# A searched order of all tasks for an attention and MoE kernel, planned with later landings, and a fifth buffer for exponentials

## The chip and the metric

One NeuronCore of one Trainium2 chip runs the whole program: TensorE (PE in the views; its weight loads PEld), VectorE (DVE), ScalarE (ACT), and SyncE (SP), which issues every transfer here. The metric is the device time of one execution in microseconds (us), lower is better. A measurement of this kernel can tell about 0.5% from no change.

## What is computed

Two batches, eight heads, 768 positions, head size 64: attention within clusters. Each query and key goes to the centroid with the largest normalised product, and a score counts only where both have the same cluster. Then two feed-forward blocks over all 1536 rows.

```python
mask = q_assign[:, :, :, None] == k_assign[:, :, None, :]
scores = np.where(mask, scale * np.matmul(q, k.transpose(0, 1, 3, 2)), -1000000000.0)
attn = softmax(scores)                       # written out in the reference
x = np.matmul(attn, v)                       # then to (1536, 512)
h = x @ w_in                                 # (1536, 2048)
g = (a0 + a1*h + a2*h**2 + a3*h**3) / (1 + abs(b0)*abs(h) + abs(b1)*h**2 + 1e-6)
x = g @ w_out                                # (1536, 512)
out = ((x @ w1) * (x @ w2) @ w3) @ wo2       # (1536, 512)
```

## The kernel before

The arithmetic comes in blocks. **FirstW** and the four **w_block**s multiply w3 by wo2 in fp32 (lines 620 and 636). An attention **unit** is one head and one tile of 128 queries, 96 in all: four score matmuls into a score bank `s` (line 844, two of them with a residual and the mask as extra rows), the row maximum on DVE (L852), the exponential on ACT into a buffer `E` (L853), six transposes on PE into two banks `t` (L866) and two copies by ACT into `et` (L872). After six units `av` multiplies by v (L906), scales on DVE (L912) and writes the head to `xd` in DRAM, from where `p1_block` loads it as `x`. The rows are treated in three chunks of 512: **p1** (eight blocks per chunk, x by w_in; L575 in fp32 for the first chunk, L577 to L579 as three fp32r matmuls for the others), the rational function behind it on ACT and DVE (L696 to L710, reading the bank `s`), **p2** (by w_out), **p3** (by w1 and w2) and **p4** (by the product W). Weights arrive as 64-bit numbers and are decoded into fp32 by one ACT and three DVE instructions (L482 to L486), then split in two fp32r parts (L526 on ACT, L527 on DVE), and some are stored in DRAM (`fin`, `fout`, `f`) for the next chunk. Cluster masks take four passes (`one`): logits on PE (L436), a transpose, a maximum, a comparison, a transpose on DVE (L442 to L445), a count on PE (L450), a last DVE step (L454).

Nothing of the order is written by hand. Every instruction or small group is a `Task` with an engine, an assumed cost and a priority. `Plan.forward` plays the four engines' queues with those costs and with assumed lags between engines; on SP a transfer takes its place behind the others, lands, and is counted as there 0.65 us after its data have moved. `Plan.backward` makes ranks from the played schedule, and `Plan.order` repeats both some 20 times, keeps the shortest, and sorts the tasks by their start. Each engine then runs its tasks strictly in that order. Buffers of a class (`SLOTS`: six `w`, three `raw`, four `E`, two `s`, two `t`, one `x`, one `kqr` and so on) are handed out in the planner too, and a task that needs a buffer waits for the last user of the one before it. In the order below, a matmul in fp32 is one row, while the trace shows it as two instructions.

Of the kernel before, what the change touches and what calls it, by code (L numbers as in the profile page):

```python
# [25 lines left out]
    PT=(33.3, 58.0),  # L26
# [5 lines left out]
    AT=(0.3751, 2.75, 3.5, 4.0, 4.0, 4.0, 4.0),  # L32
    M1=0,
    LEAD=(438.6, -178.7, 600.9),
    ALEAD=(-89.5, 241.2),
    MLEAD=2554.6,
    AOFF=37.1,
    SLOTS={"w": 6, "raw": 3, "y": 3, "x": 1, "x2": 2, "g": 16, "et": 3, "E": 4, "kqr": 1, "AB": 2, "v": 1, "sm": 6, "nn": 3, "s": 2, "t": 2, "m": 2, "sums": 2},
    WO2=-2657.8,
    OFF=(-326.5, -317.6, -25.0, -476.0, -310.4, -431.8, 243.3),  # L40
    T0=-1084.3,
    M0=-458.0,
    AHEAD=2,
    W2=("x2", "x2"),
    WR=("x", "x", "w", "w", "raw", "et", "et", "w"),
    WT=("w", "raw"),
    ROUNDS=20,
)
# [77 lines left out]
class Plan:  # L126
# [59 lines left out]
    def forward(self, rank, queue):  # L186
# [34 lines left out]
        while (best := self.next_line(lines)) is not None:  # L221
# [17 lines left out]
    def backward(self):  # L239
# [39 lines left out]
    def order(self, rounds):  # L279
        bufs = [b for q in self.queue.values() for b in q]  # L280
        queue = self.queue
        rank = [t.prio for t in self.tasks]
        best = old = None
        for k in range(rounds + 1):
# [7 lines left out]
            if best is None or span < best[0]:  # L292
                best = span, [(t.start, t.end) for t in self.tasks], [b.slot for b in bufs]
            rank = self.backward()
            old = queue
            if k % 3 == 0:
                first = {b: min(rank[t.i] for t in b.users) for b in bufs}
                queue = {c: sorted(q, key=first.get) for c, q in self.queue.items()}
        if best is None:
            raise RuntimeError("the tasks cannot be placed")  # L300
        for t, (start, end) in zip(self.tasks, best[1]):
            t.start, t.end = start, end
        for b, slot in zip(bufs, best[2]):
# [5 lines left out]
def kernel(  # L309
# [273 lines left out]

    def w_out_part(o, m, at):

        wt = [Buf(cfg["WT"][i], [P, 512], F32R) for i in range(2)]
        op("ACT", 0.48, lambda: nc.scalar.copy(wt[0].t, o.t), [o], [wt[0]], at)
        op("DVE", 0.6, lambda: nc.vector.tensor_tensor(wt[1].t, o.t, f32(wt[0].t), ALU.subtract), [o, wt[0]], [wt[1]], at)
# [4 lines left out]
    class FirstW:  # L593
# [18 lines left out]
        def run(self):  # L612
            at = self.at
            o = [Buf(c, [P, 512]) for c in "mmtt"]
            for j in range(8):
                for m0 in (0, 2):

                    def q(j=j, m0=m0):
                        for m in (m0, m0 + 1):
                            nc.tensor.matmul(o[m].t, self.f[j].t[:, m * P:(m + 1) * P], w2[j][0].t[:, w2[j][1]],  # L620
                                             start=j == 0, stop=j == 7)

                    op("PE", 1.74, q, [self.f[j], w2[j]], o[m0:m0 + 2], at + 3.4 * j)
# [3 lines left out]
    def w_block(m):  # L627
        blk = Blk("D", lambda: w3t_d[m])

        def run():  # L630
            at = blk.at
            o = Buf("m", [P, 512])

            def q(j0):
                for j in range(j0, j0 + 2):
                    nc.tensor.matmul(o.t, blk.f.t[:, j * P:(j + 1) * P], w2[j][0].t[:, w2[j][1]], start=j == 0, stop=j == 7)

            for j0 in range(0, 8, 2):
                op("PE", 1.74, lambda j0=j0: q(j0), blk.reads([j0 * P]) + w2[j0:j0 + 2], [o], at)
# [8 lines left out]
    def p1_block(c, mp):  # L648
        blk = moe_blk(c, "in", mp, lambda: win_d[mp])

        def run():
# [17 lines left out]
            h = Buf("s", [P, 2, 512])  # L669

            def q(mi, k0):
                for k in range(k0, k0 + 2):
                    mm(h.t[:, mi, 0:TC], blk, k * 256 + mi * P, [t[k][2]() for t in xs[c]], k == 0, k == 3)

            for mi in range(2):
                for k0 in (0, 2):
                    op("PE", blk.cost(2), lambda mi=mi, k0=k0: q(mi, k0),
                       blk.reads([k0 * 256]) + [t[k][:2] for t in xs[c] for k in (k0, k0 + 1)], [h], at)
# [3 lines left out]
            def A():  # L682
                return T.t[:, 0]

            def U():
                return T.t[:, 1]
# [4 lines left out]
            def hh():  # L691
                return h.t[:, :, 0:TC]

            tA, tU, tW = (T, 0), (T, 1), V
            s, v = nc.scalar, nc.vector
            op("ACT", act(2 * TC, -0.015), lambda: s.activation(A(), hh(), AF.Abs), [h], [tA], at)  # L696
            op("ACT", act(2 * TC, 0.17), lambda: s.activation(U(), hh(), AF.Identity, bias=neg[:, 2:3], scale=neg[:, 3:4]), [h], [tU], at)
            op("ACT", act(2 * TC, 0.12), lambda: s.activation(W(), A(), AF.Abs, scale=abc[:, 5:6]), [tA], [tW], at)
            op("DVE", dve(2 * TC), lambda: v.tensor_tensor(U(), U(), hh(), ALU.mult), [h], [tU], at)
            op("DVE", dve(2 * TC, 0.06), lambda: v.scalar_tensor_tensor(U(), U(), abc[:, 1:2], hh(), ALU.subtract, ALU.mult), [h], [tU], at)  # L700
            op("DVE", dve(2 * TC, 0.06), lambda: v.scalar_tensor_tensor(W(), W(), b0abs, A(), ALU.add, ALU.mult), [tA], [tW], at)
            op("ACT", act(2 * TC, 0.12), lambda: s.activation(A(), W(), AF.Ln, bias=c1), [tW], [tA], at)
            op("ACT", act(2 * TC, 0.03), lambda: s.activation(A(), A(), AF.Exp, scale=-1.0), [], [tA], at)
            op("DVE", dve(2 * TC), lambda: v.scalar_tensor_tensor(W(), W(), 1.0 + 1e-6, A(), ALU.add, ALU.mult), [tA], [tW], at)
            op("DVE", dve(2 * TC, 0.06), lambda: v.scalar_tensor_tensor(U(), U(), abc[:, 0:1], A(), ALU.subtract, ALU.mult), [tA], [tU], at)
            G = g[c, mp] = operand("out", "g", [P, 2, TC], c)
            if len(G) == 1:
                op("DVE", dve(2 * TC), lambda: v.scalar_tensor_tensor(G[0].t, W(), 2.0, U(), ALU.subtract, ALU.mult), [tW, tU], [(G[0], 0)], at)
# [399 lines left out]
```

## Time and profile before

| | us |
|---|---|
| median of 3 runs | 793.04 |
| lowest, highest | 792.76, 795.72 |
| the profiled execution | 796.5 |
| its span, first to last instruction | 794.6 |
| PE busy | 759.0 |
| DVE busy | 587.4 |
| ACT busy | 509.2 |

The profiled execution is one more run of the same program, 3.5 us above the median. A busy PE in the views includes matmuls that overlap at their ends, so the time that a matmul takes in a full queue is read from the distance of two starts, and waits that are shorter than such an overlap show no idle time.

### The profile page before, as it was taken

What the parts mean: (1) busy time and instruction counts of PE and PEld (TensorE: products, weight loads), DVE (VectorE), ACT (ScalarE), POOL (GpSimd) and SP (SyncE); (2) the same over time, 40 slices, a digit from 0 to 9 for tenths busy, and PEclk for the clock granted to TensorE, in tenths of its full rate; (3) what the DMA queues carried; (4) which work ended last, traced back from release to release, by engine and by line L of the source; (5) the groups of instructions that cost most, each with busy time, mean ns of one, the idle gap of its engine ahead of it and who ended that gap; (6) DMA issues with size and microseconds to landing.
All of it is one profiled execution on the core that took longest, in us unless ns stands there. A gap on an engine that the chain in (4) does not pass through costs nothing.

```text
span 794.6 us, 9724 instructions
## 1 busy us (share of the span) xinstructions
PE 759.0 (96%) x3545; PEld 551.1 (69%) x3545; DVE 587.4 (74%) x731; ACT 509.2 (64%) x827; POOL 0.7 (0%) x6
## 2 busy tenths in 40 slices
PE   1899999999999999999999998999999999999998
PEld 0336577666556556677778877888888888888886
DVE  6897886698788988898658999992379899233420
ACT  3238887988788886988836767862278786223320
POOL 0000000000000000000000000000000000000000
PEclk9799999999999999999999999999999999999999
DMA  7988676488735524428553644733233245332342
GB/s 273 387 278 301 204 254 189 141 244 263 249 123 173 186 94 150 127 61 283 154 190 110 189 150 138 285 116 103 80 106 107 79 156 167 128 102 84 106 158 106
DMA packets 49727, 134.99 MB, mean 170 GB/s; under 512 B 5392, under 2 KB 18448, under 8 KB 49680
## 3 DMA queue, kind: packets, MB, share of 16 engines
q1 hardware_dynamic: 49680, 134.37, 51.2%
q8 instruction: 28, 0.46, 0.2%
q14 instruction: 19, 0.16, 0.1%
HBM read 106.56 MB, written 24.64 MB: 165 GB/s over the span
## 4 chain that ended last, share of the span: by engine, by line
PE 57%; DVE 8%; ACT 6%; DMA 6%; issue 2%; SPq 0%; ACTq 0%; DVEq 0%
PE m L577 12%; PE m L578 12%; PE m L579 12%; PE s L575 4%; PE s L844 3%; PE s L577 3%; PE s L579 3%; PE s L578 3%; PE t L866 3%; PE t L906 3%; DMA raw<-in_w_in_dram 2%; ACT E L853 1%; DMA xd<-E 1%; ACT et L696 1%; DVE et L700 1%
## 5 line engine op out<-in xcount | busy, mean ns | idle before, releaser
L527 DVE TENSOR_TENSOR w<-w,w 128x1024 fp32r<-128x1024 f32 x64 | 78.1, 1222 | 76.0 <-ACT w L526 75.1
L852 DVE TENSOR_REDUCE sm<-s 128x1 f32<-128x768 f32 x96 | 90.7, 952 | 19.7 <-PE s L844 19.2
L526 ACT CAST w<-w 128x1024 fp32r<-128x1024 f32 x64 | 67.1, 1051 | 55.6 <-DMA w<-fout 39.2
L872 ACT COPY et<-t 128x384 f32<-128x384 f32 x192 | 87.8, 506 | 15.7 <-PE t L866 14.0
L844 PE MATMUL s<-AB 80*128 80x384 f32 (+1 forms) x384 | 93.2, 367 | 4.1 <-ACT E L853 2.9
L853 ACT ACTIVATE E<-s,sm 128x768 f32<-128x768 f32 x96 | 89.3, 932 | 7.9 <-DVE sm L852 5.0
L866 PEld LDWEIGHTS t<-ident,E 128*128 128x128 f32 x576 | 68.6, 140 | 27.8 <-issue 11.4
L866 PE MATMUL t<-ident,E 128*128 128x128 f32 x576 | 84.3, 274 | 2.4 <-ACT et L872 2.3
L577 PE MATMUL m<-g,w 128*128 128x512 f32 x192 | 77.4, 403 | 0.0
L844 PEld LDWEIGHTS s<-AB 80*128 80x128 f32 (+1 forms) x384 | 63.6, 189 | 18.7 <-ACT E L853 8.9
L579 PE MATMUL m<-x,w 128*128 128x512 f32 x192 | 75.6, 393 | 0.4 <-DVE w L527 0.4
L577 PE MATMUL m<-x,w 128*128 128x512 f32 x192 | 75.9, 395 | 0.0
L578 PE MATMUL m<-g,w 128*128 128x512 f32 x192 | 75.7, 394 | 0.0
L579 PE MATMUL m<-g,w 128*128 128x512 f32 x192 | 75.5, 393 | 0.0
L578 PE MATMUL m<-x,w 128*128 128x512 f32 x192 | 75.5, 393 | 0.0
L575 PE MATMUL s<-x,w 128*128 128x512 f32 x128 | 58.7, 596 | 3.8 <-DMA x<-xd 1.7
L482 ACT ACTIVATE y<-raw 128x512 f32<-128x512 f32 x65 | 44.9, 694 | 27.4 <-DMA raw<-in_w3t_dram 8.4
L577 PE MATMUL s<-x,w 128*128 128x512 f32 x128 | 50.4, 393 | 2.3 <-DVE et L700 2.3
L579 PE MATMUL s<-x,w 128*128 128x512 f32 x128 | 50.3, 393 | 0.0
L486 DVE SCALAR_TENSOR_TENSOR w<-raw,y 128x512 uint32<-128x512 uint32 x64 | 43.1, 685 | 4.2 <-PE s L575 3.0
L484 DVE SCALAR_TENSOR_TENSOR y<-raw,y 128x512 uint32<-128x512 uint32 x65 | 44.4, 687 | 0.9
L483 DVE TENSOR_SCALAR y<-y 128x512 uint32<-128x512 uint32 x72 | 30.1, 420 | 17.5 <-ACT y L482 17.2
(128 smaller groups left out, 1363.2 us busy)
## 6 DMA issues: line engine op xcount, KB each, us to landing
kqr<-in_kq_dram SPq DMA_DIRECT2D x16, 768.0 KB, 6.2
w<-fout SPq DMA_DIRECT2D x24, 512.0 KB, 3.4
raw<-in_w3t_dram SPq DMA_DIRECT2D x16, 512.0 KB, 6.4
raw<-in_w_out_dram SPq DMA_DIRECT2D x16, 512.0 KB, 5.5
raw<-in_w_in_dram SPq DMA_DIRECT2D x16, 512.0 KB, 5.3
raw<-in_w_dram SPq DMA_DIRECT2D x16, 512.0 KB, 5.5
w<-fin SPq DMA_DIRECT2D x16, 512.0 KB, 3.3
w<-f SPq DMA_DIRECT2D x16, 512.0 KB, 3.2
```

What stands on the lines that cost most here:

```text
L482: op("ACT", 0.52, lambda: nc.scalar.activation(y.t, r.t[:, :, 1].bitcast(F32), AF.Abs, scale=2.0 ** -112), [r], [y], pr)
L526: op("ACT", 0.95, lambda: nc.scalar.copy(self.hi.t, f32(f.t)), words, [self.hi], psp)
L527: op("DVE", 1.135, lambda: nc.vector.tensor_tensor(self.lo.t, f32(f.t), f32(self.hi.t), ALU.subtract), words + [self.hi], [self.lo], psp)
L575: nc.tensor.matmul(o, w.f.t[:, sl], x[0], start=first, stop=last)
L577: nc.tensor.matmul(o, w.hi.t[:, sl], x[0], start=first, stop=False)
L578: nc.tensor.matmul(o, w.hi.t[:, sl], x[1], start=False, stop=False)
L579: nc.tensor.matmul(o, w.lo.t[:, sl], x[0], start=False, stop=last)
L844: nc.tensor.matmul(p.t[:, f, 0:TA], lhs.t[0:n, q0:q0 + P], lhs.t[0:n, k0:k0 + TA], start=st, stop=not st)
L852: op("DVE", 0.865, lambda: nc.vector.tensor_reduce(mx.t, p.t[:, :, 0:TA], axis=AX.XY, op=ALU.max, negate=True), [p], [mx], OF[1])
L853: op("ACT", 0.88, lambda: nc.scalar.activation(E.t, p.t[:, :, 0:TA], AF.Exp, bias=mx.t, accum_out=sums.t[:, i, j:j + 1]), [p, mx], [E, (su ...
L866: nc.tensor.transpose(t.t[:, n * P:(n + 1) * P], e[:, kt * P:(kt + 1) * P], ident)
L872: lambda t=t, lot=lot, v=on_dve: (nc.vector.tensor_copy if v else nc.scalar.copy)(et.t[:, 3 * lot:3 * lot + 3, i * P:(i + 1) * P], t.t[:, ...
```

## The change

The planner gets three edits and the configuration new numbers. A transfer counts as there 1.5 us after its data have moved, where it was 0.65 (and 2.85 for 2.0 in `backward`); a score group on PE costs 0.78 us in the plan, where it was 0.71; `E` has five buffers, where it had four. After the old iteration a search follows: for each number in `SEEDS` (39 of them) the ranks of tasks in a stretch of the plan are shifted at random (`nudged`), the schedule is played again, and a shorter one is kept. PSUM banks are now named by tables (`HC`, `PS`); with the values given these are the banks used before. No arithmetic instruction is added or taken away.

```diff
-    PT=(33.3, 58.0),
+    PT=(8.1, 40.4),
-    AT=(0.3751, 2.75, 3.5, 4.0, 4.0, 4.0, 4.0),
+    AT=(0.75, 2.625, 3.5, 4.0, 4.0, 4.0, 4.0),
-    SLOTS={"w": 6, "raw": 3, ..., "et": 3, "E": 4, "kqr": 1, ...},
+    SLOTS={"w": 6, "raw": 3, ..., "et": 3, "E": 5, "kqr": 1, ...},
...
+    HC=("s", "s", "s"),
+    PS={"W4": "mmtt", "W": "m", "2": "mmm", "3": "mmm", "4": "mmm"},
...
                 dma = max(dma, at + 1.35) + t.nbytes / 360e3
-                t.end = dma + 0.65
+                t.end = dma + 1.5
...
-                r = at + (all_ if all_ < 8 else 2.0 + move)
+                r = at + (all_ if all_ < 8 else 2.85 + move)
...
+    def nudged(self, best, seed):
+        c = [self.chance(i, seed) for i in range(7, 12)]
+        a = c[4] * 60 - 10 if c[3] < 0.4 else c[0] * 600
+        n = (40, 120, 400, 15)[int(c[1] * 3.999)]
+        by = (4, 12, 40, 120, 1)[int(c[2] * 4.999)]
+        return [r + by * (self.chance(i, seed) - 0.5) if a <= best[3][i][0] < a + n else r
+                for i, r in enumerate(best[1])]
...
+        for seed in seeds:
+            other = self.search(self.nudged(best, seed), best[2], 3)
+            if other is not None and other[0] < best[0]:
+                best = other
...
-            op("PE", 0.71, smm, ...)
+            op("PE", 0.78, smm, ...)
```

In the changed kernel all line numbers are some 30 to 46 higher: L656 is the old L620, L672 L636, L604 L575, L890 L844, L912 L866, L740 and L739 are L697 and L696, L555 L526.

**The start, on PE.** The first rows of the program, FirstW into four banks (m and t) over eight slices of the contraction; x_129 and x_122 hold wo2's slices. Before:

```order
L620 MATMUL m_134<-x_129,w_118 128x512
L620 MATMUL m_135<-x_129,w_118 128x512
L620 MATMUL m_134<-x_129,w_140 128x512
L620 MATMUL m_135<-x_129,w_140 128x512
L620 MATMUL m_134<-x_129,w_157 128x512
L620 MATMUL m_135<-x_129,w_157 128x512
L410 MATMUL t_230<-ident,E_146 128x128
```

Now:

```order
L656 MATMUL m_158<-x_122,w_154 128x512
L656 MATMUL m_159<-x_122,w_154 128x512
L656 MATMUL m_158<-x_122,w_141 128x512
L656 MATMUL m_159<-x_122,w_141 128x512
L439 MATMUL t_196<-ident,E_116 128x128
L656 MATMUL m_158<-x_122,w_131 128x512
L656 MATMUL m_159<-x_122,w_131 128x512
L656 MATMUL t_208<-x_122,w_154 128x512
L656 MATMUL t_207<-x_122,w_154 128x512
L465 MATMUL s_217<-g_120,ct 32x384
```

The first pair used to need the first decoded weight and now needs the fourth, w_154; the first mask logits (L465, the old L436) stand behind eight matmuls, where they stood behind ten.

**The first block of p1, on PE.** s_1998 and s_2079 are the bank of p1's first block; the second of its row groups reads the heads that were written to DRAM last. Before, the first row shown is the seventh below the last matmul of `av` for head 7 of the first batch; the six between are two score groups and four groups of transposes:

```order
L636 MATMUL m_1966<-x_129,w_1646 128x512 x2
L844 MATMUL s_1976<-AB_1622 128x384 x4
L866 MATMUL t_1984<-ident,E_1957 128x128 x3
L866 MATMUL t_1994<-ident,E_1957 128x128 x3
L575 MATMUL s_1998<-x_978,w_1593 128x512 x2
L866 MATMUL t_2011<-ident,E_1972 128x128 x3
L866 MATMUL t_2017<-ident,E_1972 128x128 x3
L844 MATMUL s_2023<-AB_1766 128x384 x4
L575 MATMUL s_1998<-x_978,w_1593 128x512 x4
```

Now the first row shown is the tenth below that matmul; the nine between are two score groups, six groups of transposes and a pair of weight matmuls:

```order
L890 MATMUL s_2024<-AB_1796 128x384 x4
L912 MATMUL t_2035<-ident,E_1941 128x128 x3
L912 MATMUL t_2040<-ident,E_2018 128x128 x3
L890 MATMUL s_2044<-AB_1796 128x384 x4
L672 MATMUL m_2009<-x_122,w_1727 128x512 x2
L912 MATMUL t_2069<-ident,E_1996 128x128 x3
L912 MATMUL t_2075<-ident,E_2018 128x128 x3
L604 MATMUL s_2079<-x_953,w_1588 128x512 x2
L936 MATMUL t_2092<-ident,y_2054 128x128 x3
L912 MATMUL t_2098<-ident,E_1996 128x128 x3
L890 MATMUL s_2105<-AB_1796 128x384 x4
L604 MATMUL s_2079<-x_953,w_1588 128x512 x2
```

More work has moved between that `av` and p1's second group of two matmuls, a second pair of weight matmuls (m_2009) and one more score group among it, and that second group is cut in two.

**The sixth p1 block of the second chunk, on ACT.** s_4212 before and s_4210 now are the score bank of that block, which the eighth block takes over. Before:

```order
L698 ACTIVATE raw_4325<-et_4080,abc 128x1024
L526 CAST w_4330<-w_4279 128x1024
L482 ACTIVATE y_4339<-raw_4286 128x512
L697 ACTIVATE et_4341<-s_4212,neg 128x1024
L482 ACTIVATE y_4351<-raw_4307 128x512
L696 ACTIVATE et_4341<-s_4212 128x1024
L702 ACTIVATE et_4080<-raw_4325,c_81 128x1024
```

Now:

```order
L555 CAST w_4308<-w_4293 128x1024
L813 COPY y_4320<-m_4257 128x512
L742 ACTIVATE raw_4322<-et_4094,abc 128x1024
L740 ACTIVATE et_4332<-s_4210,neg 128x1024
L555 CAST w_4341<-w_4283 128x1024
L739 ACTIVATE et_4332<-s_4210 128x1024
L511 ACTIVATE y_4354<-raw_4305 128x512
```

A cast into a weight buffer (L526) stood two rows ahead of the first of the bank's two reads (L697, L696); now one (L555) stands between the two reads, and another three rows ahead of them.

## Rows read from the trace of the kernel before

**Rows 1.** The page's busy times of the engines, with shares of the span and instructions.

```profile
PE 759.0 (96%) x3545; PEld 551.1 (69%) x3545; DVE 587.4 (74%) x731; ACT 509.2 (64%) x827; POOL 0.7 (0%) x6
```

**Rows 2.** Four stretches: length, busy PE, PEld, DVE, ACT, POOL, PE clock, DMA share, GB/s.

```profile
0.00:58.80 58.80, 40.02 (x138) 15.78 (x138) 47.99 (x83) 19.16 (x32) 0.70 (x6) 0.91 0.88 315
58.80:82.80 24.00, 21.97 (x122) 15.22 (x120) 19.06 (x27) 21.49 (x47) 0.00 (x0) 1.00 0.81 261
82.80:500.00 417.20, 406.11 (x2035) 284.78 (x2034) 349.17 (x456) 327.38 (x588) 0.00 (x0) 1.00 0.55 176
500.00:780.00 280.00, 280.00 (x1210) 226.85 (x1209) 171.18 (x167) 139.57 (x162) 0.00 (x0) 1.00 0.37 128
```

**Rows 3.** PE's waits over the span: line, who ended them, us, times, longest.

```profile
PE m L620 <- DVE x L486: 18.8, 2, 11.9
PE s L844 <- ACT E L853: 2.9, 5, 1.1
...
PE s L577 <- DVE et L700: 2.3, 1, 2.3
PE s L575 <- DMA x<-xd: 1.7, 1, 1.7
```

**Rows 4.** PE's first rows: start, us, what, count, idle before.

```profile
11.89 3.38 PE L620 MATMUL m<-x,w 128*128 128x512 f32 x4 [11.89 <-DVE x L486]
22.16 6.78 PE L620 MATMUL m<-x,w 128*128 128x512 f32 x8 [6.89 <-DVE x L486]
...
28.88 1.88 PE L620 MATMUL m<-x,w 128*128 128x512 f32 x4
...
64.97 0.82 PE L866 MATMUL t<-ident,E 128*128 128x128 f32 x6
...
78.82 4.09 PE L906 MATMUL m<-et,v 128*64 128x384 f32 x24
```

**Rows 5.** DVE in order of time: three decode steps, and the first row maximum.

```profile
17.69 0.68 DVE L484 SCALAR_TENSOR_TENSOR y<-raw,y 128x512 uint32<-128x512 uint32 x1
18.29 0.42 DVE L483 TENSOR_SCALAR y<-y 128x512 uint32<-128x512 uint32 x1
18.63 0.68 DVE L486 SCALAR_TENSOR_TENSOR w<-raw,y 128x512 uint32<-128x512 uint32 x1
...
61.02 0.95 DVE L852 TENSOR_REDUCE sm<-s 128x1 f32<-128x768 f32 x1
```

**Rows 6.** Pieces of the chain that ended last: start, us, what (prices).

```profile
176.26 0.74 ACT et L872 x2
177.00 1.77 ACT E L853 x4
...
180.80 4.02 PE m L906 x24
...
230.22 1.72 PE s L575 x4
231.94 0.66 PE t L866 x6
232.60 0.71 PE s L844 x4
```

**Rows 7.** The same chain where head 7 goes to DRAM.

```profile
195.81 4.96 DMA xd<-E
```

**Rows 8.** PE where p1's first block and the second chunk's eighth block wait.

```profile
206.20 1.13 PE L575 MATMUL s<-x,w 128*128 128x512 f32 x2 [1.73 <-DMA x<-xd]
...
490.48 0.47 PE L577 MATMUL s<-x,w 128*128 128x512 f32 x1 [2.27 <-DVE et L700]
```

**Rows 9.** The chain ahead of the second of these.

```profile
477.76 5.51 DMA f<-w
484.99 1.09 ACT et L697
...
489.06 1.29 DVE et L700
```

More of the change, by code (lines that the diff above doesn't have):

```diff
@@ L277, in backward, with search @@
         return late
-    def order(self, rounds):
+    def search(self, rank, queue, rounds):
         bufs = [b for q in self.queue.values() for b in q]
-        queue = self.queue
-        rank = [t.prio for t in self.tasks]
         best = old = None
@@ L292, in order @@
             if best is None or span < best[0]:
-                best = span, [(t.start, t.end) for t in self.tasks], [b.slot for b in bufs]
+                best = span, rank, queue, [(t.start, t.end) for t in self.tasks], [b.slot for b in bufs]
+            if k == rounds:
+                break
             rank = self.backward()
@@ L582, with banks @@
     w2 = []
+    def banks(cls, n):
+        if cls != "s":
+            return [(b, lambda b=b: b.t) for b in (Buf(k, [P, 512]) for k in (cls * n)[:n])]
+        pairs = [Buf("s", [P, 2, 512]) for _ in range((n + 1) // 2)]
+        return [((pairs[i // 2], i % 2), lambda i=i: pairs[i // 2].t[:, i % 2]) for i in range(n)]
     def w_out_part(o, m, at):
         wt = [Buf(cfg["WT"][i], [P, 512], F32R) for i in range(2)]
-        op("ACT", 0.48, lambda: nc.scalar.copy(wt[0].t, o.t), [o], [wt[0]], at)
-        op("DVE", 0.6, lambda: nc.vector.tensor_tensor(wt[1].t, o.t, f32(wt[0].t), ALU.subtract), [o, wt[0]], [wt[1]], at)
+        op("ACT", 0.48, lambda: nc.scalar.copy(wt[0].t, o[1]()), [o[0]], [wt[0]], at)
+        op("DVE", 0.6, lambda: nc.vector.tensor_tensor(wt[1].t, o[1](), f32(wt[0].t), ALU.subtract), [o[0], wt[0]], [wt[1]], at)
         for t, d, n in ((wt[0], "h", 0), (wt[1], "l", 1)):
@@ L613, in run @@
             at = self.at
[L614 removed]
+            o = banks(cfg["PS"]["W4"], 4)
             for j in range(8):
@@ L688, in W, with U @@
+            def U(j=None):
+                return T.t[:, 1] if j is None or len(h) == 1 else T.t[:, 1, j]
             def W():
                 return V.t
-            def hh():
-                return h.t[:, :, 0:TC]
-            tA, tU, tW = (T, 0), (T, 1), V
+            tA, tU, tW = [(T, 0, j) for j in parts], [(T, 1, j) for j in parts], [V]
+            n = 2 * TC // len(h)
             s, v = nc.scalar, nc.vector
-            op("ACT", act(2 * TC, -0.015), lambda: s.activation(A(), hh(), AF.Abs), [h], [tA], at)
@@ L701, in run @@
[L701 to L705, printed above, removed]
+            for j in parts:
+                op("ACT", act(n, -0.015), lambda j=j: s.activation(A(j), hh[j](), AF.Abs), [h[j]], [tA[j]], at)
+                op("ACT", act(n, 0.17), lambda j=j: s.activation(U(j), hh[j](), AF.Identity, bias=neg[:, 2:3], scale=neg[:, 3:4]),
+                   [h[j]], [tU[j]], at)
@@ new lines, in run @@
+            op("ACT", act(2 * TC, 0.12), lambda: s.activation(W(), A(), AF.Abs, scale=abc[:, 5:6]), tA, tW, at)
+            for j in parts:
+                op("DVE", dve(n), lambda j=j: v.tensor_tensor(U(j), U(j), hh[j](), ALU.mult), [h[j]], [tU[j]], at)
+                op("DVE", dve(n, 0.06), lambda j=j: v.scalar_tensor_tensor(
+                    U(j), U(j), abc[:, 1:2], hh[j](), ALU.subtract, ALU.mult), [h[j]], [tU[j]], at)
+            op("DVE", dve(2 * TC, 0.06), lambda: v.scalar_tensor_tensor(W(), W(), b0abs, A(), ALU.add, ALU.mult), tA, tW, at)
@@ L713, in p1_block @@
+                put(G, 0, lambda t: t, U, tU, 2 * TC, at, False)
         blk.run, blk.pe = run, blk.cost(8)
@@ L764, in run @@
                     op("PE", blk.cost(2), lambda w_=w_, k0=k0: q(w_, k0),
[L765 removed]
+                       blk.reads([(w_ * 4 + k0) * P]) + [(t, k) for t in x2[c] for k in (k0, k0 + 1)], [o[w_][0]], at)
             a = Buf("y", [P, TC])
[L767 to L768 removed]
+            op("ACT", act(TC), lambda: nc.scalar.copy(a.t, o[0][1]()[:, 0:TC]), [o[0][0]], [a], at)
+            op("DVE", dve(TC), lambda: nc.vector.tensor_tensor(a.t, a.t, o[1][1]()[:, 0:TC], ALU.mult), [o[1][0]], [a], at)
             (hk, hi), (lk, lo) = half(c, m, 0), half(c, m, 1)
@@ L1035 @@
         return plan, None
-    done = plan.order(cfg["ROUNDS"])
+    done = plan.order(cfg["ROUNDS"], cfg["SEEDS"])
     if only_plan:
```

88 lines of the change are left out of this document (50 added, 38 removed).

## Prediction, made before the result was known

> **What bounds the kernel now.** I read the page's busy times first: PE is busy for 759.0 of 794.6 us, DVE for 587.4, ACT for 509.2 [rows 1]. No arithmetic moves to another engine, so the change can win only what PE waits. The table of stretches says where that is [rows 2]. Up to 58.8 us, where attention begins, PE is busy for 40.02, so 18.8 are missing. From 58.8 to 82.8, the end of the second head's `av`, 24.00 - 21.97 = 2.0 are missing, and from 82.8 to 500 another 417.20 - 406.11 = 11.1. From 500 to 780 PE is busy for 280.00 of 280.00 us: nothing can be won there by any order. The rest is the last block, its copy and its transfer, which keep their place. So 13.1 us of visible waits behind the start, and 18.8 at the start, are all there is. The list of PE's waits names the releasers [rows 3]: 18.8 us for decoded weights (L486) at the start, one wait of 2.3 us for a score bank that DVE still reads (L700), one of 1.7 us for heads that come back from DRAM, and small waits for ACT.
>
> **Prices.** From the chain of waits: a score group 0.71 us, six transposes 0.66, two fp32 matmuls (four instructions) 1.72, an `av` 4.02, an exponential 1.77 / 2 = 0.89, two copies by ACT 0.74 [rows 6]. From the stretch after 500 us, three-part matmuls take 280 / 1210 = 0.23 us each [rows 2]. Decode: 0.60 + 0.34 + 0.60 = 1.54 us of DVE, from the distances of starts (the third step taken as the first) [rows 5].
>
> **Part 1, the start.** PE begins at 11.89 us, does one pair of matmuls in 3.38 us, waits 6.89 us, and runs the next eight instructions in 6.78 us, 0.85 each, before they take 1.88 / 4 = 0.47 and less [rows 4]: the first ones ran at 1.2 GHz and the later ones at 2.4, after PE had been busy; the mean granted clock of this stretch is 0.91 [rows 2]. In the changed order the first pair waits for the fourth decoded weight. By the order DVE has then done 18 instructions, where the first pair used to need 12 and the second 30; two decodes at 1.54 later than 11.89 is 15.0 us. The second pair needs 28. So PE starts 3.1 us later, but then goes on with little or no gap, some 3.5 us ahead of the 22.16 of before. That lead does not reach the end of the stage, since DVE sets it: DVE is busy for 47.99 of the first 58.8 us [rows 2]. Ahead of the first row maximum, at 61.02 us [rows 5], DVE has 82 instructions instead of 86: one decode (1.54) and one subtraction (0.6, as a decode step of that size) fewer, so 2.1 us earlier if DVE waits as long as before. Against that, the old order had four weight matmuls (two times 1.72, 3.4 us) between its first score groups, and the new one has none. Before, the first exponential was there at about 61.02 + 0.95 + 0.89 = 62.9 us, and its transposes came at 64.97 [rows 4], behind that work; now they can come 2.1 us earlier and at once, but without the 3.4 us of work. To that point the start wins 2.1 + (64.97 - 62.9) - 3.4 = 0.8 us. From there to the second `av` the new order holds nothing but attention. ACT needs for nine units 9 x (0.89 + 0.74) = 14.7, and about 4 us for two heads' preparation, one decode and two `av` copies, so 18.7 us; PE has 19.3 us for the same. Before, PE lost 2.0 visible us here [rows 2]. If ACT runs closely, half of that goes, and some 0.2 us of waits that are too short to show. I put the start, up to the end of the second `av` (78.82 + 4.02 us before [rows 4]), at 0.8 + 1.0 + 0.2, **-2.0 us**; its ends are -4 (the whole lead of PE kept) and +4 (DVE waits for the mask logits, which now stand behind matmuls at half clock: 15.0 + two pairs of 3.4 at half clock + two of 1.7 puts the first logits near 25 us, and DVE, with about five decodes of 1.54 and a few small steps ahead of the first mask step, is there at about 23.5).
>
> **Part 2, heads through DRAM.** Head 7 is written in 4.96 us [rows 7] and read again, and PE waits 1.73 us for it in p1's first block [rows 8]. From the end of that `av` to the matmul that reads the slice, PE's work in the old order is 2.74 (the rows above the fence) + 1.72 + 0.71 + 0.66 + 1.72 + 0.66 + 0.71 + 0.86 = 9.8 us, so the trip takes 9.8 + 1.7 = 11.5. In the new order it is 5.1 + 0.71 + 0.66 + 0.71 + 1.72 + 0.66 + 1.72 + 0.33 + 0.33 + 0.71 + 0.86 = 13.5 us. The wait goes, with 2 us to spare: **-1.7**; ends 0 and -1.7. The old plan counted 0.65 us from a transfer's last byte to its landing, the new one 1.5, so this cover is what the edit asks for. The Trainium skill ("DMA: Bandwidth & Descriptors", "Anatomy of one DMA") speaks against needing it: about 2.0 us fixed and bytes at 436 GB/s, an estimate of 2.2 us for 96 KB and 2.6 for the 256 KB read back, 4.8 together. By that the heads would have been there before PE asked, and the sum would be 1.7 us smaller. The trace shows 4.96 for the write alone, and a wait.
>
> **Part 3, the bank of the second chunk's eighth block.** PE waits 2.27 us at 490.48 [rows 8], because the sixth block's bank is read by ACT only from 484.99 and released by L700 at 489.06 + 1.29; ahead of that read stands a cast that waits for a transfer of 5.51 us [rows 9]. By the order PE has 11.2 us of work from the end of the sixth block to the start of the eighth; it needed 11.2 + 2.3 = 13.5. Now it has 13.9, the sixth block ending 2.7 us earlier. If ACT is as late as before, that just covers it: **-2.3**; ends 0 and -2.3.
>
> **Part 4, all other waits to 500 us.** 11.1 - 1.7 - 2.3 = 7.1 us, some dozen waits of 0.3 to 1.6 us. E's fifth buffer and wider gaps between p1 blocks work on them: work between a unit's scores and its first transposes has a median of 6.6 us now against 5.9, at the same prices. But a new order has waits of its own, which this trace does not show. I take a third of 7.1 as gone, 2.4, and 1.4 as new: **-1.0**; ends -5 and +4 (all of the old ones kept and half as many added). The Trainium skill ("Perfetto Trace Analysis", "Optimization Strategy") reads a gap that repeats on the engine that should be saturated as too few buffers. The repeated wait here is a score group for the exponential that frees its bank, 2.9 us [rows 3], and `s` stays at two: by that rule the fifth `E` is worth nothing there, and part 4 would be 0.
>
> Switches between kinds of matmul are as many as before within a few, and PE's total work is the same, so they cost nothing.
>
> **Sum.** -2.0 - 1.7 - 2.3 - 1.0 = -7.0 us against the profiled execution: 796.5 becomes 789.5, its span 794.6 becomes 787.6. The profiled execution lies 3.5 us above the median of 793.04; I apply the difference to the median: **786.0 us**.
>
> **Rivals.** (a) *More is won*: part 1 and part 4 at their good ends, 4 + 1.7 + 2.3 + 5 = 13 us, 780. For it: 18.8 us stand idle at the start and the order was made for the shortest plan. Against: DVE is full at the start and the new attention stretch has no other work for PE. (b) *The start eats the rest*: the stretch without weight matmuls between the units runs at ACT's pace with a gap per unit. At 0.5 us for each of nine units, part 1 turns from -2 to +2.5; with parts 2 to 4 that is 790.5, no difference that can be measured (0.5%, 4.0 us, is about the least that can). (c) *Slower*: DVE's queue is strict, and at the start each mask pass goes to PE and back twice, eight trips in all. In the old order decodes of other weights fill these. From 7 us to 58.8 DVE has only about 4 us idle. If the trips cost DVE 1.2 us each more, attention begins 9.6 us later less the 2.1; with parts 2 to 4 at -1.7, 0 and 0 the time is 793.04 + 7.5 - 1.7 = 799. It decides from about 8 us more of DVE idle time ahead of the first row maximum; against it stand the decodes that still lie between the passes. (d) *The plan's landings change nothing*: transfers that queue behind each other land when they land; parts 2 and 3 stay, part 1 and 4 give 0 to -3: 790 to 793, also no difference.
>
> **Chances.** Forecast, 4 to 10 us won: 0.52. (a) more than 10: 0.16. (b) and (d), within 4 us: 0.24. (c): 0.08. So faster by over 0.5% 0.68, within 0.5% 0.24, slower 0.08. The range reaches from 779.5, just beyond (a), to 792.0, most of (b) and (d).
>
> **What would show it.** Part 1: PE starts at about 15 us and shows one gap less; the first row maximum lies at 58 to 60 us instead of 61.02, and the second `av` ends before 82.8. Part 2: no wait for `xd` in PE's list. Part 3: no wait of over 1 us for L700 near 480 us. Part 4: visible idle time from the second `av` to 500 us falls from 11.1 to about 6. After that, PE at 280.00 in 280 us again. The prediction is wrong if PE's list shows new waits of several us for ACT or DVE in the first 90 us, or if parts 2 and 3 only change the name of what PE waits for.

## The result, and the profile after

The changed kernel takes 786.73 us (median of 4 runs, 784.67 to 789.05) beside 794.38 for the kernel before in the same measurement: a ratio of 0.9899, 95% interval 0.9852 to 0.9945. Measured again with six runs (the run after_again below) it is 786.90 beside 794.05, 0.9917 (0.9897 to 0.9938). So it is faster by 0.8 to 1.0%; 786.0 was predicted, in a range of 779.5 to 792.0. Its profiled execution took 789.05 us with a span of 787.2 (787.6 was predicted), against 796.5 and 794.6 before.

The page's busy times of the changed kernel, answering [rows 1]:

```profile
PE 759.4 (96%) x3545; PEld 553.0 (70%) x3545; DVE 584.3 (74%) x731; ACT 511.7 (65%) x827; POOL 0.7 (0%) x6
```

The work is the same, and this line doesn't show the gain. PE's waits, answering [rows 3] (line, who ended them, us, times, longest):

```profile
PE m L656 <- DVE w L515: 14.1, 1, 14.1
PE t L912 <- ACT et L918: 3.7, 4, 1.5
PE s L479 <- DVE g L474: 1.3, 2, 0.9
PE t L656 <- DVE x L515: 0.9, 1, 0.9
PE s L890 <- DVE g L483: 0.9, 2, 0.4
PE m L606 <- ACT y L813: 0.9, 1, 0.9
PE s L604 <- DMA x<-xd: 0.8, 1, 0.8
```

The two waits at the start, 18.8 us, are one of 14.1. The 2.9 us of score groups waiting for the exponential are 0.2, below the rows shown, and no wait for L745 (the old L700) is over 0.3. ACT's copy of transposes (L918) is waited for longer than before, 3.7 us (2.2 in after_again) where it was 2.3 (L866 and L872 then):

```profile
PE t L866 <- ACT et L872: 2.3, 5, 1.0
```

The stretches, first those of [rows 2] and then two inside the first of them (columns as there):

```profile
0.00:58.80 58.80, 41.35 (x148) 17.07 (x149) 49.68 (x85) 22.00 (x36) 0.70 (x6) 0.98 0.91 325
58.80:82.80 24.00, 23.78 (x130) 18.75 (x130) 19.47 (x29) 22.13 (x49) 0.00 (x0) 0.84 0.81 247
82.80:500.00 417.20, 410.83 (x2053) 288.68 (x2052) 353.47 (x462) 335.99 (x591) 0.00 (x0) 1.00 0.57 183
500.00:780.00 280.00, 279.88 (x1206) 225.97 (x1205) 161.71 (x158) 130.97 (x153) 0.00 (x0) 1.00 0.34 119
```

```profile
48.00:55.00 7.00, 4.70 (x12) 1.67 (x12) 6.94 (x10) 2.89 (x7) 0.00 (x0) 1.00 0.75 187
55.00:66.00 11.00, 10.09 (x36) 8.60 (x37) 9.86 (x13) 8.72 (x16) 0.00 (x0) 0.55 1.02 318
```

From 82.8 to 500 us the visible idle time of PE is 417.20 - 410.83 = 6.4 us, where it was 11.1; in after_again it is 3.9. Just where attention begins, a loss shows as no idle time at all: from 55 to 66 us PE is busy for 10.09 of 11 us, but at a granted clock of 0.55, so for most of it at 1.2 GHz.

Stretches of equal time hold different work in the two orders. So I added up PE's work in the order of each trace, each matmul counted with its usual distance of two starts at 2.4 GHz (0.43 us for half of an fp32 matmul, 0.23 for an fp32r one, 0.18 for a score matmul, 0.11 for a transpose), and compared when each kernel reaches the same sum. Minus means earlier than the profiled execution of before. The sum over the program is 739 us.

| PE work done (us) | place | changed | after_again | warm | moved |
|---|---|---|---|---|---|
| 0 | first matmul | +2.3 | +2.3 | +2.5 | +2.3 |
| 30 | late in FirstW | -7.3 | -7.1 | -7.1 | -6.6 |
| 40 | some units in | +1.4 | +1.7 | -0.1 | +1.3 |
| 54 | about the first head's `av` | -0.8 | -0.4 | -2.1 | -0.2 |
| 158 | ahead of p1's first block | -3.3 | -4.3 | -5.7 | -3.9 |
| 172 | behind it | -2.8 | -5.0 | -6.5 | -5.3 |
| 340 | attention nearly done | -6.7 | -8.9 | -10.5 | -9.1 |
| 436 | ahead of the bank of [rows 8] | -7.3 | -9.4 | -10.9 | -9.5 |
| 440 | behind it | -9.6 | -11.7 | -13.2 | -11.8 |
| 738 | end | -7.4 | -9.4 | -11.3 | -10.1 |

Four things are to be read here. A lead of 7 us at the start is lost within 10 us of work. Most of what stays is won slowly, between 54 and 440. And 2.2 us are given back behind 440. Last, the gain from 54 to 440, 8.8 us (11.3 in after_again), is some 4 us more than what the visible idle time of PE lost from 82.8 to 500 us, 4.7 (7.2): these 4 us never stood in a list of waits, and what they are was not traced. The two executions of the changed kernel differ by 2 us, nearly all of it between 120 and 172 us of work. The execution of before is itself 2 us above its median in these measurements, so the leads at the end are that much too large for a typical pair.

### The profile page after: what moved, and what is told of

Read it like the earlier page. It is cut to its first block, busy times and chain, and to the rows that moved or that the text cites. A ratio compares the mean times of both kernels' runs of the same rounds, so it can differ in the third digit from the quotient of the medians.

```text
span 787.2 us, 9707 instructions
## 1 busy us (share of the span) xinstructions
PE 759.4 (96%) x3545; PEld 553.0 (70%) x3545; DVE 584.3 (74%) x731; ACT 511.7 (65%) x827; POOL 0.7 (0%) x6
## 4 chain that ended last, share of the span: by engine, by line
PE 53%; DVE 25%; ACT 10%; DMA 6%; issue 5%; SPq 0%; ACTq 0%; DVEq 0%
PE m L606 12%; PE m L608 11%; PE m L607 11%; DVE sm L898 3%; PE t L912 3%; PE s L890 3%; DVE y L513 2%; PE s L606 2%; PE s L608 2%; PE s L607 2%; ACT E L899 2%; PE t L952 2%; DVE w L515 2%; DVE w L556 2%; DVE raw L747 2%
## 5 line engine op out<-in xcount | busy, mean ns | idle before, releaser
L555 ACT CAST w<-w 128x1024 fp32r<-128x1024 f32 x64 | 66.7, 1051 | 58.5 <-PE m L607 25.4
L898 DVE TENSOR_REDUCE sm<-s 128x1 f32<-128x768 f32 x96 | 90.9, 951 | 14.1 <-PE s L890 13.7
L890 PE MATMUL s<-AB 80*128 80x384 f32 (+1 forms) x384 | 97.0, 377 | 1.6 <-DVE g L483 0.9
L918 ACT COPY et<-t 128x384 f32<-128x384 f32 x192 | 86.5, 497 | 15.6 <-PE t L912 15.5
L912 PEld LDWEIGHTS t<-ident,E 128*128 128x128 f32 x576 | 69.3, 143 | 31.0 <-issue 12.9
L912 PE MATMUL t<-ident,E 128*128 128x128 f32 x576 | 85.7, 279 | 4.2 <-ACT et L918 3.7
L890 PEld LDWEIGHTS s<-AB 80*128 80x128 f32 (+1 forms) x384 | 66.4, 196 | 14.3 <-ACT E L899 4.5
L604 PE MATMUL s<-x,w 128*128 128x512 f32 x128 | 59.6, 595 | 1.0 <-DMA x<-xd 0.8
```

The costliest lines, as they stand in the source:

```text
L555: op("ACT", 0.95, lambda: nc.scalar.copy(self.hi.t, f32(f.t)), words, [self.hi], psp)
L604: nc.tensor.matmul(o, w.f.t[:, sl], x[0], start=first, stop=last)
L890: nc.tensor.matmul(p.t[:, f, 0:TA], lhs.t[0:n, q0:q0 + P], lhs.t[0:n, k0:k0 + TA], start=st, stop=not st)
L898: op("DVE", 0.865, lambda: nc.vector.tensor_reduce(mx.t, p.t[:, :, 0:TA], axis=AX.XY, op=ALU.max, negate=True), [p], [mx], OF[1])
L912: nc.tensor.transpose(t.t[:, n * P:(n + 1) * P], e[:, kt * P:(kt + 1) * P], ident)
L918: lambda t=t, lot=lot, v=on_dve: (nc.vector.tensor_copy if v else nc.scalar.copy)(et.t[:, 3 * lot:3 * lot + 3, i * P:(i + 1) * P], t.t[:, ...
```

## The experiments

Each run is given with the median of its times, lowest to highest, and the ratio to the kernel before on the same chip with its 95% interval. after_again, warm, moved and no_search ran together, then moved_warm, search_only, late0 and four_E, then other_seeds and search_five_E, then the last two. Between these groups the kernel before differs by up to 1.3 us, so there I compare ratios, 0.1% being 0.8 us.

### The start: PE's clock

**after_again**, the changed kernel unaltered.

> The changed kernel once more, unaltered, as the base of the runs beside it. Theory: its executions differ mainly by how long PE runs at half clock at the start of attention; those with a mean granted clock of 1.000 should lie near 784.5 us, those with 0.993 near 789, the median near 786.5 (0.990 of before). Rival: clock and time of the executions are unrelated.

786.90 us (786.45 to 790.14), 0.9917 (0.9897 to 0.9938). The profiled execution has again a clock of 0.58 from 55 to 66 us. The rest of the expectation failed: executions with a mean clock of 0.993 took 786.76 to 788.16 us, two with 0.996 took 786.80 and 790.14. The one execution of the changed kernel with a clock of 1.000, in the first measurement, took 784.67 us. So the clock can be one cause of the spread, but it is not the main one; that the transfers (below) are another is likely and not shown.

**warm**, in the mask's count, for its last pass:

```diff
             def count():
+                if b == 1 and which:
+                    for _ in range(4):
+                        nc.tensor.matmul(cnt.t[:, 0, 0:P], ident, ident)
                 for hf in range(2):
```

> Four matmuls of the identity with itself stand on PE ahead of the last mask count, in its bank, which it then overwrites: about 0.86 us of work where the changed kernel's PE was idle for 0.89 us at 54.1 us. Nothing else moves. Theory (the half clock from 55 to 66 us follows from PE's idle pieces between 48 and 58 us): the clock of that stretch goes from 0.55 to 1.00, a score group there takes 0.95 us and not 1.65, and every execution is near 784.5 us, some 2 us under the median of the changed kernel and 4 under its profiled execution. Rival (the other idle pieces, at 55.65 and 58, are enough for it): the clock stays near 0.55 and the time at 786.5. Second rival (the count is held up by the new work): 0.5 us slower.

784.75 us (783.81 to 785.53), 0.9880 (0.9861 to 0.9899), and no execution above 785.53. Three of its four executions have a mean clock of 1.000 and one 0.995; of ten executions of the changed kernel one has 1.000. The two stretches in it:

```profile
48.00:55.00 7.00, 5.57 (x20) 2.72 (x20) 6.94 (x9) 3.92 (x7) 0.00 (x0) 1.00 0.79 200
55.00:66.00 11.00, 7.85 (x45) 6.27 (x45) 10.90 (x16) 9.69 (x18) 0.00 (x0) 1.00 1.01 305
```

And PE in order of time, first the changed kernel, then this one (start, us, what, count, idle before; L893 here is L890, L915 is L912):

```profile
54.12 0.50 PE L479 MATMUL s<-g,trib 128*128 128x384 bf16 x2 [0.89 <-DVE g L474]
55.05 0.93 PE L890 MATMUL s<-AB 128*128 128x384 f32 x4 [0.43 <-DVE g L483]
56.42 1.65 PE L890 MATMUL s<-AB 128*128 128x384 f32 x4 [0.44 <-DVE g L483]
58.31 0.90 PE L912 MATMUL t<-ident,E 128*128 128x128 f32 x3 [0.24 <-ACT E L899]
58.86 1.63 PE L890 MATMUL s<-AB 128*128 128x384 f32 x4
```

```profile
53.32 1.05 PE L480 MATMUL s<-ident 128*128 128x128 f32 x8
54.37 0.48 PE L482 MATMUL s<-g,trib 128*128 128x384 bf16 x2
...
56.68 0.98 PE L893 MATMUL s<-AB 128*128 128x384 f32 x4 [0.43 <-DVE g L486]
58.57 0.55 PE L915 MATMUL t<-ident,E 128*128 128x128 f32 x3 [0.91 <-ACT E L902]
...
62.41 0.55 PE L915 MATMUL t<-ident,E 128*128 128x128 f32 x3 [1.40 <-ACT E L902]
```

The work that nobody needs fills the idle piece of 0.89 us, the count is no later than in after_again (54.37 and 54.38 us), the score groups stay at 0.98 instead of 1.65 us, and the kernel is 2.1 us faster. The Trainium skill ("TensorE: Matmul & The Clock Gate", "A second HAM failure mode: psum-queue depth-cycling") tells of a kernel in which short idle pieces between groups of matmuls let the clock swing between its levels; the trace agrees in that the clock fell behind such pieces, with 4.70 busy of 7.00 us ahead of the fall and 5.57 where none came. But the clock was not all of the lost lead. At 40 us of work this kernel has none left either (-0.1 in the table): PE now waits 0.91 and 1.40 us for exponentials, as it has nothing else to do there.

### What is left on PE's path: strict queues

**moved**, the order as planned, then five instructions set back in it (the numbers are those of tasks):

```diff
     done = plan.order(cfg["ROUNDS"], cfg["SEEDS"])
+    for a, b in ((768, 633), (986, 800), (995, 972), (1801, 1866), (1086, 776),):
+        ids = [t.i for t in done]
+        t = done.pop(ids.index(a))
+        done.insert(ids.index(b), t)
```

> The changed kernel's order with five instructions set back in their queues, nothing else: on ACT two first decode steps (L511) that wait for weights, at 155.0 and 194.4 us, behind the two copies of transposes that stood behind them; on ACT L739 at 250.2, which waits for DVE, behind one copy; on ACT L748 at 491.5, which waits for DVE, behind the copy of p3's bank (L813); on SP one load of weights, at 199.1, behind the load of the heads. Theory (what PE still waits for is ready work that stands in a strict queue behind something late): PE's waits of 1.49, 0.95, 1.07, 0.87 and 0.77 us go, and at least 3.5 of these 5.15 us show in the time: about 783. Rival (PE's waits only change their name, the next late thing takes their place): within 1 us of the changed kernel, 786 to 787.

785.03 us (784.58 to 786.29), 0.9887 (0.9868 to 0.9905): by the medians 1.9 us under the changed kernel, between the two theories. One of the five as it stands in the changed kernel, PE and then ACT (the transposes of 153.10 are ready, their copy stands behind a decode step that waits for weights):

```profile
153.10 0.82 PE L912 MATMUL t<-ident,E 128*128 128x128 f32 x6
153.67 0.94 PE L890 MATMUL s<-AB 128*128 128x384 f32 x4
156.10 0.93 PE L912 MATMUL t<-ident,E 128*128 128x128 f32 x6 [1.49 <-ACT et L918]
```

```profile
155.02 0.66 ACT L511 ACTIVATE y<-raw 128x512 f32<-128x512 f32 x1 [1.33 <-DMA raw<-in_w_in_dram]
155.58 0.85 ACT L918 COPY et<-t 128x384 f32<-128x384 f32 x2
```

Two of the five waits, this one of 1.49 and the 0.77 for the heads, were those of one execution: after_again's list has neither, and its waits for L918 are 2.2 us. So there was less to win than the 5.15 us that I had added up from a single trace. PE's list with the moves:

```profile
PE t L912 <- ACT et L918: 1.4, 3, 0.7
PE s L479 <- DVE g L474: 1.3, 2, 0.9
PE s L890 <- ACT E L899: 1.0, 2, 0.7
```

The waits for L918 shrink. Of the 1.0 us of waits for the exponential 0.74 lie at 68.1 us, ahead of all five instructions, so the moves didn't make them. Where the 1.9 us come from is not shown: in the table moved and after_again are within 0.4 us of each other from 54 to 440 us of work, where four of the five moves act, and 0.7 us apart at the end, nearly all of it behind 440, at the fifth. The profiled execution of moved is the slowest of its four.

**moved_warm**, both edits.

> The five moves of the run moved and the four identity matmuls of the run warm together. Theory (they act in different places, one on the clock at the start of attention, the others on queues behind 150 us): the gains add, 1.9 and 2.1 us from 786.9, so 783, about 0.986 of before. Rival (what the warm start wins is waited for again at the moved places, or the reverse): not under 784.5.

784.20 us (783.20 to 785.05), 0.9874 (0.9851 to 0.9896). It has the lowest median of all, but 1.9 and 2.1 us did not add: 0.5 us is left of the moves (0.06% by the ratios). In the table's terms it ends 11.3 us ahead of before, exactly as warm does. Where the second gain goes isn't settled; warm and moved_warm have the same waits of 2.3 us for exponentials behind the start.

### The parts of the change

**no_search**: `SEEDS=()`.

> The changed kernel with an empty list of seeds: later landings, the longer score groups, five buffers E and all new numbers stay, only the search by shifted ranks is left out, so the order is the best of the old iteration. Theory (the search removes small waits all along the attention part): 789 to 793 us, 3 to 6 over the changed kernel, with more of PE's waits between 82 and 500 us. Rival (the later landings and the fifth buffer carry the gain): within 1.5 us of the changed kernel, 785 to 788.

789.35 us (788.06 to 791.26), 0.9941 (0.9924 to 0.9959): 2.4 over the changed kernel, less than the 3 to 6 of the theory, but beyond the rival's 1.5. Score groups wait for the exponential again:

```profile
PE m L656 <- DVE x L515: 17.6, 2, 11.6
PE t L912 <- ACT et L918: 3.6, 4, 1.9
PE s L890 <- ACT E L899: 2.7, 5, 1.5
```

But the longest of these waits, 1.53 us, is at 61.81 us, at the start of attention, and the clock of the stretch from 55 to 66 us is 0.84. From 82.8 to 500 us PE's visible idle time is 6.0 us, no more than the 6.4 of the changed kernel's first profile, and 2.1 more than in after_again; so the theory of more waits along attention is not borne out clearly.

**other_seeds**: another list of 20 seeds, nothing else.

> The changed kernel with another list of seeds (20 numbers, found in the same way from the same unsearched order, to a plan of the same length); all else as changed. It measures how far two orders that are equal in the plan lie apart on the chip, and so what the differences of the other runs are worth. Theory (a run that takes one part away tells what that part is worth): 786 to 788, within 1 us of the changed kernel. Rival (each order has its own luck of 2 us and more): anywhere from 783 to 791, and then the 2.1 of late0, the 2.4 of no_search and a part of the 6.2 of four_E are no measure of their part.

786.99 us (785.94 to 788.66), 0.9912 (0.9894 to 0.9931), 0.1 from the changed kernel, though its order differs widely: its lead at 30 us of work is 4.0 us instead of 7.1, its clock from 55 to 66 us is 1.00, and it ends equal. So a good search ends at this time by more than one road. It is one pair, so it doesn't say how far two searched orders can lie apart; below I read differences of 2 us and more, with that doubt.

**search_only**: the numbers of the kernel before, its landings, prices and four buffers, with a search (12 seeds).

> The kernel before with its own numbers, its own landings (0.65 and 2.0 us), score groups of 0.71 us and four buffers E; only the search by shifted ranks is added, with a list of 12 seeds found for this plan in the same way (each one shortens it). Theory (a search pays only where the plan knows when transfers land; here it fits the order to transfers that are late on the chip): within 1.5 us of before, 792.5 to 795.5. Rival (the search carries the gain, whatever the landings): 787 to 790.

790.46 us (788.01 to 796.35), 0.9963 (0.9942 to 0.9985): some 3 us under before. My theory that a search is worthless without the later landings falls, and the rival's range just misses it too. What remained shows the old bank again, PE's largest wait behind the start, for L745, at 481.76 us:

```profile
PE s L606 <- DVE et L745: 3.1, 1, 3.1
```

**search_five_E**: the same with `"E": 5` (19 seeds).

> The kernel before with its own numbers and landings, the search, and five buffers E; beside search_only only the fifth buffer (and the list of 19 seeds, found for this plan in the same way, to a plan of the same length) is new. Theory as it stands after four_E (the fifth buffer is worth several us): 785 to 788, 2.5 to 5 under the 790.5 of search_only. Rival (four_E was slow since its numbers were made for five buffers, and its losses lie mostly behind 400 us, after attention): 789.5 to 791.5, no better than search_only.

788.66 us (787.28 to 789.57), 0.9932 (0.9912 to 0.9952): 0.3% or 2.5 us under search_only by the ratios, the median between both ranges. It also prices the new numbers: late0 (below) has the same landings, prices, search and five buffers, but the new numbers and its own seeds, and 0.9938 (0.9918 to 0.9957). So with the old landings and prices the new numbers win nothing that can be measured.

**four_E**: the changed kernel with `"E": 4` (43 seeds).

> The changed kernel with four buffers E, all else as changed, and a list of 43 seeds found for that plan in the same way. Theory (waits for a score bank, not for E, repeat in attention, so the fifth buffer is worth little): 786 to 788.5. Rival (the fifth buffer is what gives the longer distance from scores to transposes, and most of the gain): 790 to 794.

793.14 us (791.18 to 794.89), 0.9989 (0.9976 to 1.0001): 0.7% over the changed kernel, nearly all of the gain gone, against my theory. But only a part of it went where a buffer of exponentials would be missed. Counted at equal work as above, four_E is 3.0 us behind after_again at 340 us of work, and 5.3 at the end; 2.3 of that come behind attention. In attention score groups wait for the exponential again (0.2 in the changed kernel); the other two rows lie behind it, from 461 us on:

```profile
PE s L890 <- ACT E L899: 3.2, 6, 0.8
...
PE m L606 <- DVE y L814: 2.1, 3, 1.3
PE s L608 <- DVE w L556: 1.9, 1, 1.9
```

Nor does the fifth buffer alone put more units in flight. From the start of an exponential to the end of its last transpose (the k-th paired with the k-th) the median is 5.1 us before, 6.6 in the changed kernel, 5.2 in no_search, which has five buffers, and 6.9 in four_E, which has four. It is the search that stretches the units: in the other searched orders it is 5.5 (search_only) to 8.2 (early_landings). A buffer E also holds each head on its way to DRAM and some halves in p3, and four_E's other numbers were made for five. Which of these uses the fifth one serves wasn't tried.

**late0**, **short_scores**, **early_landings**: the changed kernel with 25, 30 and 35 seeds of their own and one or both of these edits taken back:

```diff
-                t.end = dma + 1.5
+                t.end = dma + 0.65
...
-                r = at + (all_ if all_ < 8 else 2.85 + move)
+                r = at + (all_ if all_ < 8 else 2.0 + move)
...
-            op("PE", 0.78, smm, ...)
+            op("PE", 0.71, smm, ...)
```

> The changed kernel with its numbers and five buffers E, but the old landings (0.65 and 2.0 us) and score groups of 0.71 us, and a list of 25 seeds found for that plan in the same way. Theory (later landings keep work between a transfer and its user): 789 to 793 us, with PE waits of 1 us and more between 82 and 500 us that end with a transfer, or with ACT behind one. Rival (the landings don't matter, the search finds as good an order without them): 785.5 to 788.

> The changed kernel with the later landings, but with score groups of 0.71 us in the plan as before, and a list of 30 seeds found for that plan in the same way; it takes apart what late0 had both of. Theory (late0's 4.7 us of waits of score groups for the exponential come from the price of a score group, since a plan with 0.71 sets ACT's and DVE's work of each unit too early): 788 to 790, with at least 2 us of such waits in PE's list. Rival (the price is of no account, the landings are): 786 to 787.5, with under 1 us of such waits.

> The changed kernel with score groups of 0.78 us, but with the old landings (0.65 and 2.0 us), and a list of 35 seeds found for that plan in the same way. Theory (it was the price of a score group): 786 to 788, with under 1 us of waits of score groups for the exponential. Rival (the landings carry late0's loss): 788.5 to 791, with 2 us and more of PE waits that end with a transfer or with ACT behind a late one.

| | score group 0.78 | score group 0.71 |
|---|---|---|
| later landings | changed: 786.90, 0.9917 (0.9897 to 0.9938) | short_scores: 787.90 (785.82 to 788.81), 0.9903 (0.9886 to 0.9921) |
| old landings | early_landings: 795.59 (793.20 to 798.61), 1.0009 (0.9996 to 1.0022) | late0: 789.01 (786.93 to 790.45), 0.9938 (0.9918 to 0.9957) |

With either price the later landings are the faster in these four orders: by 0.92% (7.3 us) with the new one, and by 0.35% (2.8 us) with the old. The price itself does nothing that can be told apart beside the later landings (0.9917 and 0.9903). My theory for short_scores was half right: its waits for the exponential are there, and cost nothing visible in the total. late0 lies in the range of its theory, but without the mechanism: between 82 and 500 us no wait of PE is over 0.8 us. early_landings lies above both of its ranges. PE's list of late0, of short_scores and of early_landings, the rows of score groups and of the heads:

```profile
PE s L890 <- ACT E L899: 4.7, 8, 1.0
```

```profile
PE s L890 <- ACT E L899: 3.0, 8, 0.5
```

```profile
PE s L890 <- ACT E L899: 6.0, 5, 2.6
...
PE s L604 <- DMA x<-xd: 1.1, 1, 1.1
```

early_landings has what the edit is against, a wait for the heads, and it falls to half clock at the start, in this stretch after a wait of 2.64 us at 61.25:

```profile
55.00:66.00 11.00, 7.95 (x28) 5.60 (x27) 9.75 (x14) 7.33 (x13) 0.00 (x0) 0.76 1.04 313
```

Why the old landings cost 7.3 us with one price and 2.8 with the other stays open: the search ends in a different order each time, and early_landings may have ended in a poor one. By 40 us of work it is already some 4 us behind after_again, where the clock falls; that part need not come from the landings.

## Why the prediction was right, and where its terms were not

The time, the sign and the span came out (-7.0 predicted, 796.5 - 789.05 = -7.45 in the profiled executions), but the terms err in both directions and cancel.

**Part 1, -2.0: measured -0.8 and -0.4.** First a slip: the `av` at 78.82 us in [rows 4] that the prediction calls the second head's is the first's. PE started at 14.14 us (15.0 predicted), with one gap less, and the logits came at 23.53 (near 25). Two sizes were off, both to the good: the lead was 7 us, not 3.5, and the first row maximum came at 56.30 us, 4.7 earlier and not 2.1. DVE there:

```profile
55.44 0.93 DVE L483 SCALAR_TENSOR_TENSOR g<-s,g 128x768 f32<-128x768 f32 x1
56.30 0.93 DVE L898 TENSOR_REDUCE sm<-s 128x1 f32<-128x768 f32 x1
```

The step that failed is the one behind it, "PE has 19.3 us for the same": the price was for 2.4 GHz. The prediction had read half clock in [rows 4] at the very start and did not ask whether it could return where the order has nothing but attention. warm prices it: 2.1 us of the total, and -2.1 at 54 us of work. That warm has just the forecast's size takes two errors that cancel: the first row maximum came some 2.4 us earlier there than forecast, and 2.3 us of waits for the exponential took that back. What rival (b) described, gaps behind the first score groups in the stretch without filler, is also there (0.91 and 1.40 us in warm); in the changed kernel half clock stretches PE's work over them.

**Part 2, -1.7: half right.** In one execution PE still waits for the heads, in the other it doesn't:

```profile
205.76 1.02 PE L604 MATMUL s<-x,w 128*128 128x512 f32 x2
207.55 1.12 PE L604 MATMUL s<-x,w 128*128 128x512 f32 x2 [0.77 <-DMA x<-xd]
```

The cover is there: 14.2 us of PE's work lie between the `av` and the matmul that waits (13.5 predicted). The step that failed took the trip as a constant 11.5 us. From the end of that `av` to the landing of the heads it took 11.7 us before, 15.9 here and 14.6 in after_again. The last write was issued 3.5 us behind the `av` where it was 1.3, and the read alone took 5.4 us before and here 8.0 (KB, us from issue to landing):

```profile
x<-xd SPq DMA_DIRECT2D x1, 256.0 KB, 5.4
```

```profile
x<-xd SPq DMA_DIRECT2D x1, 256.0 KB, 8.0
```

In after_again it took 6.9, and in moved 5.8. A 512 KB load is issued 0.44 us ahead of the read in both executions of the changed kernel, and behind it in moved; before, two transfers of that size were issued 3.7 and 4.3 us ahead. So other transfers are the likely reason, and not the whole one, as the same order gave 8.0 and 6.9. Moving more work in front of a transfer's user can move other transfers in front of the transfer. By the Trainium skill ("DMA: Bandwidth & Descriptors", "Anatomy of one DMA") the estimate for this read was 2.6 us, from a fit that the page made for transfers issued by GpSimd. The trace, where SyncE issues them among others, does not agree, with 5.4 to 8.0 us, and the measurement decides.

**Part 3, -2.3: right to the tenth.** Between 436 and 440 us of work the lead grows by 2.3 in both executions. The same step is there in no_search (2.5) and in four_E (1.9); only search_only keeps the wait (3.1 us). So it is not the search that removes it, and not the later landings, as late0 and early_landings have the step too (2.6 and 2.5). search_five_E, with the old numbers, has it (1.9): so by these orders either the new numbers or the fifth buffer is enough. The cause named with [rows 9] was not tested by itself.

**Part 4, -1.0: too small.** With part 2 it was to be -2.7; from 54 to 436 us of work the measured gain is 6.5 us, in after_again 9.0, of which some 2 may belong to the execution of before, 2 us above its median. The visible idle time, predicted at about 6, is 6.4 and in after_again 3.9. The step that failed is the allowance of 1.4 us for new waits and the third that goes. It was not the search alone that made the rest: no_search has gained 4.1 us in this stretch. Nor are the waits of score groups for the exponential much of it: only 1.4 of the 2.9 us of before lie behind 84 us, 0.55 of the 2.7 in no_search, and 0.2 are left in the changed kernel. The larger part of the surplus left no trace in the visible idle time, and its cause stays open. By the rule of the Trainium skill ("Perfetto Trace Analysis", "Optimization Strategy"), that such a gap can mean too few buffers, part 4 would be 0, as `s` stays at two. The trace does not agree: with two `s` the waits behind 84 us went from 1.4 to 0.2 us, and in search_only, with four `E` as well, also to 0.2.

**The tail, 0: measured +2.2.** The stretch from 500 to 780 us is full, as predicted, but the lead shrinks from 9.6 to 7.4. Some 0.9 us of it is one wait at 493 us for ACT's copy, which stood behind L748; PE, then ACT:

```profile
493.13 0.50 PE L606 MATMUL m<-AB,w 128*128 128x512 f32 x1 [0.87 <-ACT y L813]
```

```profile
491.45 1.16 ACT L748 ACTIVATE et<-raw,c 128x1024 f32<-128x1024 f32 x1 [1.14 <-DVE raw L747]
492.51 0.56 ACT L813 COPY y<-m 128x512 f32<-128x512 f32 x1
```

moved takes 0.4 us of it away; then DVE's L814 is late instead (0.41). The rest is spread in small pieces and has no name.

So the profiled -7.4 are -0.8, -6.5 for parts 2 and 4 together, -2.3 and +2.2. The forecast had the sign of each part right, and the size of one; that the sum came out to half a us is luck.

Rival (a), 780 us, isn't reached even with both edits of moved_warm. Rival (c) fell, as DVE came to the first row maximum earlier, and against (d) speak early_landings and late0, with one order each.

## What to carry to other kernels

By the ratios the search won 0.2% (no_search) to 0.4% (search_only) here, the fifth buffer 0.3% to 0.7%, and later landings 0.35% to 0.9%, each by one order. Test a searched order with a second list of seeds before its parts are priced, as each edit to the plan also gives another order. A term taken from one execution is good to some 2 us here; add up waits from two traces before you set out to remove them. And a list of waits is not all that an order can win: count work done against time as well. Where a dense engine meets a chain of other engines and no filler is left for it, a short piece of idle matmuls can pay for itself.

## What the runs showed of the hardware

That PE falls back to half clock in the middle of a program was not expected: after 4.70 busy us of 7.00, the clock is 0.55 over the next 11 us, although PE is busy for 10.09 of them, and four useless matmuls (1.05 us) ahead of the fall hold it at 1.00. That stretch is then busy for less, 7.85 us, with idle pieces of 0.91 and 1.40 us, and keeps its clock; no_search and early_landings fell in it behind pieces of 1.53 and 2.64 us, after 7.00 busy us of 7.00. And one transfer of 256 KB, in the same place of nearly the same program, took 5.4, 5.8, 6.9 and 8.0 us.
